# Attention with 64-key blocks for 58 queries, and reciprocals spread as three bf16 parts

## The chip, the cores and the metric

The kernel runs on one core of a Trainium2 chip. The metric is the device time of one execution in microseconds (us). Fast executions of one kernel mostly agree within 1 to 2%; some fall into a slower state. The profile shows one execution on its engines: PE is the matrix engine (TensorE), PEld its weight loads, DVE is VectorE, ACT ScalarE, POOL GpSimd, SP the engine that issues loads.

## The reference

Attention over batch 8, 8 heads, 576 positions, head size 64, in two forms whose results are added. One attends in full on positions averaged four by four (144 of them); the other only to neighbours less than four positions away. The sum, as 4608 rows of 512, goes through a two-layer network with a SiLU between.

```python
out_d = sm_attn(q_d, k_d, v_d)                 # q_d, k_d, v_d: means of 4 positions
out_up = np.repeat(out_d, factor, axis=2)      # factor = 4
mask = np.abs(pos[:, None] - pos[None, :]) < factor
scores = np.where(mask, scale * np.matmul(q, k.transpose(0, 1, 3, 2)), -1e9)
out_local = np.matmul(softmax(scores), v)      # (cut: the softmax is written out)
x = (out_up + out_local) as [4608, 512]        # (cut: transpose and reshape)
h = x @ w_in                                   # 512 -> 2048
return (h * (1.0 / (1.0 + np.exp(-h)))) @ w_out
```

## The kernel before

Heads are handled in 32 pairs. The local band of a head is cut into key blocks of 64, each of which serves 48 queries, six blocks for half a head. All products of attention are 64x64 matmuls on quarters of the array (64*64 in the profile, where the network's have 128*128). A "visit" `V(n)` holds everything that TensorE does for attention between two portions of the network:

```python
def V(n):                                  # cut to its order
    pe_cross(u, pv, z)                     # PV of pair n-2 and Z of pair n-1: parts across halves
    pe_S(u, n)                             # scores of pair n
    pe_T(u, n + 1)                         # transposes of pair n+1
    pe_main(u, pv, z)                      # Z of pair n-1, then PV of pair n-2
    after_T(n + 1); after_PV(pv); after_Z(z); after_S(n)   # work of the other engines

for i in range(6):                         # in pe_S; the values (PV) have the same six blocks
    for h in range(2):
        for y in range(2):
            t = 288 * y + 48 * i
            mm(u, AB[half(y), h, 48 * i:48 * i + 48], kT[j][half(h), t:t + 64],
               qT[j][half(h), t:t + 48], rl, [rAB[h]])
```

Z, the denominators, are collected 36 columns at a time in rows of a bank. VectorE takes their reciprocal, and each row must then be spread over the 64 partitions of a head. The first four pairs (`NDIR = 4`) do it with matmuls (`RB`), all later ones by a round trip: written to DRAM, then read back twice, each read repeating one row over 64 partitions. ScalarE issues both steps, so it waits in its own stream until the write has landed before it can issue the reads (5.7 us for pair 4).

```python
def after_Z(p):
    one("DVE", f"r{p}", 0.75, lambda e: e.reciprocal(zr[i][:, :, :], CD[:, :, 360:396]), ...)
    if p < NDIR:
        return
    dma("ACT", f"z{p}", scr[u][:, :], zr[i]..., ...)          # write
    for h in range(2):
        dma("ACT", f"b{p}", Rb[u][half(h), :], src, ...)      # read, stride 0 over 64 partitions

def RB(p):
    for x in range(2):
        for m in range(10):                # float32 matmul against a selector
            mm(u, HP[:, x, 36 * m:36 * m + 36], sel[:, m, :], zr[i][:, x, :], ...)
    one("ACT", f"eb{p}", 0.8, ...)         # copy HP to Rb
```

The reciprocal, the copies out of PSUM, `th` (a tanh by ScalarE) and `gT` (its product by VectorE) all belong to chains that TensorE waits for: each g1 matmul group (four matmuls of the input layer) writes one of two banks `HP`, which is free again when `th` and `gT` have read it.

The softmax here doesn't subtract the row's maximum and nothing guards it: scores larger than these inputs give would overflow.

## Time and profile before

| | before |
|---|---|
| median (lowest to highest of 3) | 436.39 us (433.86 to 438.46) |
| profiled execution | 444.3 us, span 442.6, granted clock 0.942, of the slow state |
| matmuls of one visit | 160 |
| matmuls of RB, four pairs | 160 recorded passes, 35.0 us busy |
| instruction queue (queue 8) | 51 packets, 0.84 MB, so 16 KB each; TensorE has 13,090 recorded instructions (6530 matmuls, 6560 weight loads), 257 a packet: an instruction block |

The span is read in four stages, because each has another limit: up to the first g1 (65.9 us), then to the Z of the tenth visit (50.7), to the Z of the last pair (235.3), and the tail of the network alone (90.7). The lines are in the prediction.

### The profile page before, as it was taken

What the parts mean: (1) busy time and instruction counts of PE and PEld (TensorE: products, weight loads), DVE (VectorE), ACT (ScalarE), POOL (GpSimd) and SP (SyncE); (2) the same over time, 40 slices, a digit from 0 to 9 for tenths busy, and PEclk for the clock granted to TensorE, in tenths of its full rate; (3) what the DMA queues carried; (4) which work ended last, traced back from release to release, by engine and by line L of the source; (5) the groups of instructions that cost most, each with busy time, mean ns of one, the idle gap of its engine ahead of it and who ended that gap; (6) DMA issues with size and microseconds to landing.
All of it is one profiled execution on the core that took longest, in us unless ns stands there. A gap on an engine that the chain in (4) does not pass through costs nothing.

```text
span 442.6 us, 14638 instructions
## 1 busy us (share of the span) xinstructions
PE 384.9 (87%) x6530; PEld 265.3 (60%) x6560; DVE 221.0 (50%) x355; ACT 169.1 (38%) x290; POOL 166.2 (38%) x207
## 2 busy tenths in 40 slices
PE   2799987974597887969797989799999999999997
PEld 1799985653464554646465656466666656666653
DVE  5532125576555464656464656566776543433420
ACT  4221024532244251524344445354545434343421
POOL 9441224356634444445354545445632120000000
PEclk9999999889589896969698999999999999999999
DMA  8999909978997474746575767583131210110111
GB/s 224 262 275 279 211 8 204 254 184 238 215 269 208 125 219 123 198 141 187 146 191 160 204 185 221 152 209 111 67 97 63 87 62 28 43 49 24 49 47 71
DMA packets 87258, 67.35 MB, mean 152 GB/s; under 512 B 59036, under 2 KB 68764, under 8 KB 87196
## 3 DMA queue, kind: packets, MB, share of 16 engines
q1 hardware_dynamic: 74460, 48.77, 41.9%
q10 hardware_dynamic: 8512, 11.36, 9.1%
q0 software_dynamic: 4224, 6.29, 6.6%
q8 instruction: 51, 0.84, 0.8%
q14 instruction: 11, 0.09, 0.1%
HBM read 58.03 MB, written 10.47 MB: 155 GB/s over the span
## 4 chain that ended last, share of the span: by engine, by line
PE 82%; issue 7%; DMA 4%; DVE 2%; ACT 2%; ACTq 1%; SPq 0%; DVEq 0%
PE HP L336 40%; PE o L336 23%; PE CD L336 8%; PE pe_ L336 6%; DMA scr<-zr 2%; PE AB L336 2%; PE pe_ L526 1%; DMA Rb<-scr 1%; DMA qk<-in_k_dram 1%; ACTq L425 1%; PE o L526 1%; ACT th L738 1%; DVE zr L666 1%; DVE gT L740 0%; SPq L425 0%
## 5 line engine op out<-in xcount | busy, mean ns | idle before, releaser
L336 PE MATMUL HP<-xT,w_in_sb 128*128 128x512 f32 x576 | 177.7, 447 | 2.7 <-DVE gT L740 2.3
L740 DVE SCALAR_TENSOR_TENSOR gT<-th,HP 128x512 bf16<-128x512 f32 x144 | 97.1, 685 | 119.3 <-ACT th L738 118.8
L738 ACT ACTIVATE th<-HP 128x512 f32<-128x512 f32 x144 | 85.8, 598 | 160.1 <-PE HP L336 150.1
L336 PEld LDWEIGHTS HP<-xT,w_in_sb 128*128 128x128 f32 x576 | 114.4, 204 | 34.1 <-DVE gT L740 3.2
L336 PE MATMUL o<-w_out_bf,gT 128*128 128x512 bf16 x437 | 106.4, 386 | 2.5 <-issue 1.0
L336 PEld LDWEIGHTS o<-w_out_bf,gT 128*128 128x128 bf16 x464 | 42.0, 100 | 60.0 <-issue 17.6
L722 POOL TENSOR_TENSOR xT<-xo 128x576 fp32r<-128x576 f32 (+3 forms) x48 | 45.0, 950 | 74.0 <-DVE xo L695 74.0
L508 POOL CAST vb<-vs 128x768 bf16<-128x768 f32 x32 | 26.4, 826 | 97.5 <-PE CD L336 88.5
L666 DVE RECIPROCAL zr<-CD 128x72 f32<-128x72 f32 x32 | 19.4, 607 | 50.9 <-PE CD L336 50.9
L502 POOL CAST qkb<-qk 128x1152 bf16<-128x1152 f32 x30 | 34.4, 1146 | 25.1 <-PE pe_ L526 13.2
L336 PE MATMUL CD<-Pt,vb 64*64 64x48 bf16 x768 | 14.8, 196 | 24.7 <-issue 24.4
L336 PE MATMUL HP<-zr,gT 128*128 128x36 f32 x160 | 35.0, 408 | 0.2 <-DVE zr L666 0.2
L336 PEld LDWEIGHTS HP<-zr,gT 128*128 128x128 f32 x160 | 34.4, 332 | 0.6 <-DVE zr L666 0.3
L695 DVE TENSOR_TENSOR xo<-CD,Rb 128x720 f32<-128x720 f32 x32 | 28.7, 898 | 11.7 <-PE CD L336 9.7
L513 POOL TENSOR_TENSOR vt<-vq 128x512 f32<-128x512 f32 x24 | 30.8, 1283 | 0.0
L536 ACT ACTIVATE kT<-pe_ 128x576 bf16<-128x576 bf16 x32 | 20.8, 650 | 18.9 <-PE pe_ L526 11.2
L755 ACT ACTIVATE osb<-o 128x512 f32<-128x512 f32 x29 | 17.4, 599 | 26.4 <-PE o L336 26.2
L336 PEld LDWEIGHTS CD<-Pt,vb 64*64 64x64 bf16 x768 | 11.1, 117 | 26.5 <-issue 25.4
L336 PE MATMUL pe_<-w_out_bf,gT 128*128 128x512 bf16 x109 | 26.1, 380 | 0.2
L540 DVE TENSOR_REDUCE kd<-kT 128x144 bf16<-128x576 bf16 x32 | 23.6, 738 | 1.7 <-ACT kT L536 1.7
L526 PE MATMUL o<-idn,qkb 64*64 64x64 bf16 x576 | 17.8, 206 | 7.6 <-DVE qkb L497 6.0
L543 DVE TENSOR_REDUCE qd<-qT 128x144 bf16<-128x576 bf16 x32 | 23.8, 743 | 1.3 <-ACT qT L339 1.2
(69 smaller groups left out, 358.3 us busy)
## 6 DMA issues: line engine op xcount, KB each, us to landing
vs<-in_v_dram SPq DMA_DIRECT2D x126, 96.0 KB, 4.1
Rb<-scr ACTq DMA_DIRECT2D x56, 180.0 KB, 4.1
qk<-in_q_dram SPq DMA_DIRECT2D x32, 288.0 KB, 5.5
out_dram<-osb SPq DMA_DIRECT2D x36, 256.0 KB, 2.3
qk<-in_k_dram SPq DMA_DIRECT2D x31, 288.0 KB, 6.0
vq<-in_v_dram SPq DMA_DIRECT2D x24, 256.0 KB
w_in_sb<-in_moe_w_in_dram POOLq DMA_DIRECT2D x4, 1024.0 KB, 10.0
w_out_bf<-in_moe_w_out_dram POOLq DMA_DIRECT2D x4, 512.0 KB, 9.9
```

The lines of the kernel that those rows point to most:

```text
L336: L.op(u, lambda t: t.matmul(out_, lhsT, rhs, start=start, stop=stop, skip_group_check=True), r, w)
L502: one("POOL", f"c{p}", 1.15, lambda g: g.tensor_copy(qkb[j][:, :, :], qk[i][:, :, :]), r=[R(f"qk{i}0"), R(f"qk{i}1")], w=[R(f"qkb{j}0"), R ...
L508: one("POOL", f"cw{p}", 0.85, lambda g: g.tensor_copy(vb[m][:, :, :], vs[i][:, :, :]), r=rr, w=[R(f"vb{m}")])
L513: one("POOL", f"va{p}", 1.3, lambda g: g.tensor_tensor(vt[:, :, :], vq[i][:, :, 0:128], vq[i][:, :, 128:256], ALU.add), r=rr, w=[R("vt")])
L526: L.op(u, lambda e, o=o, w=w, j=j: e.transpose(o, w, idn[half(j), :]), [R("id"), R(f"qkb{n}{x}")], [rE if x else rF])
L540: one("DVE", f"mk{p}", 0.74, lambda e: e.tensor_reduce(kd[j][:, 0:SD], kT[j][:, 8:584].rearrange("p (g r) -> p g r", r=4), AX.X, ALU.add), ...
L543: one("DVE", f"mq{p}", 0.74, lambda e: e.tensor_reduce(qd[j][:, :], qT[j][:, :].rearrange("p (g r) -> p g r", r=4), AX.X, ALU.add), r=[R(f ...
L666: one("DVE", f"r{p}", 0.75, lambda e: e.reciprocal(zr[i][:, :, :], CD[:, :, 360:396]), r=rCD, w=[R(f"zr{i}")], prio=-4)
L695: one("DVE", f"m{p}", 0.92, lambda e: e.tensor_tensor(xo[x][:, :, :].rearrange("p x (m n) -> p x m n", n=36), CD[:, :, 0:360].rearrange("p ...
L722: one("POOL", f"a{p}", 0.15 + n * 0.0019, lambda g, dst=dst, in0=in0, in1=in1: g.tensor_tensor(dst, in0, in1, ALU.add), r=[R(f"xo{x}")], w ...
L738: one("ACT", f"t{j}_{f}", 0.62, lambda e: e.activation(th[tb][:, :], hps[hb], AF.Tanh, scale=0.5), r=[rH[hb]], w=[R(f"th{tb}")], prio=-1)
L740: one("DVE", f"s{j}_{f}", 0.71, lambda e: e.scalar_tensor_tensor(gT[j % 2][:, f, :], th[tb][:, :], 1.0, hps[hb], ALU.add, ALU.mult), r=[rH ...
```

## The change

Its intent is fewer instructions on TensorE, and no float32 matmuls. A key block of 64 can serve 58 queries (three neighbours on each side), so five blocks do instead of six: a visit has 4 matmuls fewer for scores and 4 fewer for values. Z is collected 72 columns at a time instead of 36, 28 matmuls fewer: 124 a visit, not 160. The reciprocal then has 144 columns instead of 72. RB writes the reciprocal as a sum of three bf16 numbers and spreads each with a bf16 selector.

```diff
-            for i in range(6):                      # pe_S; PV likewise
+            for i in range(5):
-                        t = 288 * y + 48 * i
-                        mm(u, AB[half(y), h, 48 * i:48 * i + 48], kT[j][half(h), t:t + 64],
-                           qT[j][half(h), t:t + 48], rl, [rAB[h]])
+                        c, n = 58 * i, 58 if i < 4 else 56
+                        t = 288 * y + c
+                        mm(u, AB[half(y), h, c:c + n], kT[j][half(h), t:t + 64],
+                           qT[j][half(h), t:t + n], rl, [rAB[h]])
 ...
-                for s in range(8):                  # Z in pe_main; the other Z parts likewise
+                for s in range(4):
-                            mm(u, CD[half(h), j, 360:396], ..., Pt[m][half(j), h, 36 * s:36 * s + 36], ...)
+                            mm(u, CD[half(h), j, 360:432], ..., Pt[m][half(j), h, 72 * s:72 * s + 72], ...)
 ...
-            ... e.reciprocal(zr[i][:, :, :], CD[:, :, 360:396])
+            ... e.reciprocal(zr[i][:, :, :], CD[:, :, 360:432])
             if p < NDIR:
+                rh: h = bf16(zf);  rx: rest = zf - h;  rm: m = bf16(rest);  rl: l = bf16(rest - m)   # four DVE ops
                 return
 ...
-            for x in range(2):                      # RB
-                for m in range(10):
-                    mm(u, HP[:, x, 36 * m:36 * m + 36], sel[:, m, :], zr[i][:, x, :], ...)
+            for m in range(5):
+                x, c = divmod(m, 3)
+                for a in range(3):
+                    mm(u, HP[:, x, 144 * c:144 * c + 144], sel[:, m, :], rpart[a], ...,
+                       start=a == 0, stop=a == 2)
```

Cut: the windows in which values are loaded (80 KB instead of 96), masks, constants (their fills moved from GpSimd to VectorE), the value sums of a pair on TensorE (`VP`, 14 matmuls instead of 16), two value casts moved to ScalarE, and the estimated costs that the kernel's own scheduler orders by.

## The prediction

> **What bounds the kernel now.** I read the page first (busy shares, slices, the chain), then the groups of matmuls by form, the list of waits, the busy times by stage, and last the timeline of TensorE around two visits. A "visit" is the block of small 64x64 matmuls for attention: scores of one pair, transposes of the next, denominators (Z) of the one before and values (PV) of the one before that. From the tenth visit on, four groups of input-layer matmuls (g1) and four of output-layer matmuls (g2) stand between visits.
>
> The page: TensorE is busy 87% of the span, and the chain that ended last is 82% TensorE with 7.2% "issue", time in which nothing that the profile shows was waited for. The three rows of section 2 say when: TensorE is full in the tail, but near the middle has slices of 4 to 8 and a granted clock of 5 to 9.
>
> ```profile
> PE 384.9 (87%) x6530; PEld 265.3 (60%) x6560; DVE 221.0 (50%) x355; ACT 169.1 (38%) x290; POOL 166.2 (38%) x207
> PE   2799987974597887969797989799999999999997
> PEclk9999999889589896969698999999999999999999
> q8 instruction: 51, 0.84, 0.8%
> PE 82%; issue 7%; DMA 4%; DVE 2%; ACT 2%; ACTq 1%; SPq 0%; DVEq 0%
> L336 PE MATMUL HP<-zr,gT 128*128 128x36 f32 x160 | 35.0, 408 | 0.2 <-DVE zr L666 0.2
> L336 PEld LDWEIGHTS HP<-zr,gT 128*128 128x128 f32 x160 | 34.4, 332 | 0.6 <-DVE zr L666 0.3
> ```
>
> The last two rows are the spreading of the first four pairs' reciprocals (RB): 160 float32 passes, 35 us, with no wait. The stage view (columns: length, then busy us of PE, PEld, DVE, ACT, POOL, clock, DMA share, GB/s) cuts the span at the first g1 (65.9), at the Z of the tenth visit (116.6) and at the Z of the last pair (351.9):
>
> ```profile
> 0.00:65.90 65.90, 53.42 (x937) 50.42 (x937) 22.39 (x41) 15.18 (x24) 26.80 (x59) 1.00 0.93 211
> 65.90:116.60 50.70, 36.06 (x1011) 27.43 (x1008) 31.38 (x55) 20.87 (x37) 29.51 (x31) 0.85 0.96 221
> 116.60:351.90 235.30, 208.55 (x4114) 136.20 (x4128) 136.89 (x216) 100.35 (x175) 107.42 (x117) 0.92 0.58 161
> 351.90:442.60 90.70, 86.90 (x492) 51.22 (x500) 30.30 (x44) 32.66 (x55) 2.44 (x2) 1.00 0.13 49
> ```
>
> Then the gaps. Two rows of the list of waits:
>
> ```profile
> PEld CD L336 <- issue: 28.5, 17, 4.6
> PE CD L336 <- issue: 24.4, 9, 4.5
> ```
>
> and the timeline of one visit with a gap in it (start, duration, instruction, wait before it):
>
> ```profile
> 212.01 0.30 PE L336 MATMUL CD<-Pt,vb 64*64 64x48 bf16 x14
> 215.04 0.36 PE L336 MATMUL CD<-Pt,vb 64*64 64x48 bf16 x10 [2.73 <-issue]
> 215.18 0.36 PE L336 MATMUL CD<-Pd,vd 64*64 64x72 bf16 x8
> 215.46 3.78 PE L336 MATMUL HP<-xT,w_in_sb 128*128 128x512 f32 x8
> ```
>
> The reader is to see a run of equal matmuls broken in the middle, with no semaphore involved, and the eight g1 matmuls after it at 3.71 us on the chain instead of 1.85 us. Such gaps begin at 141.3, 164.4, 188.6, 212.3, 235.8, 257.8, 277.7 and 298.6 us, always 766 recorded TensorE instructions apart, and sum to 22.6 us. Z to Z, visits alternate between 8.9 us (no gap) and 11 to 15.4 us. So stage 3 is not bound by matmuls: its 22 visits would take 22 x 8.9 = 196 us, and it takes 235.
>
> [...] 766 is three blocks, and in the gap at 212.31 the packet starts at 212.39, takes 1.03 us, and TensorE goes on at 215.04. [...]
>
> **The change, part by part.**
>
> *RB in bf16.* Removed: 4 x 40 float32 passes at 217 ns = 4 x 8.7 us, all on the path between 15 and 62 us. Added: 4 x 15 bf16 matmuls of 144 columns, [...] 1.8 to 3 us per pair. TensorE is given back about 25 us. VectorE gets a reciprocal of 144 columns: [...] 1.08 us, so 0.5 us more; and four small operations of about 0.25 us, 1 us a pair. Then the chain of a pair binds: Z, reciprocal, PV, multiply on the same two banks take about 0.5 + 1.1 + 0.5 + 0.9 us [...], and the VectorE sum of a pair is about 5.6 us (two reductions 1.5, mask 0.45, reciprocal 1.1, parts 1.0, two value copies 0.6, multiply 0.9). I take 6.5 us a pair. First Z at about 14 us as before (two value casts moved to ScalarE may make it wait for their loads; the constants come earlier), fourth Z at 33.5, then reciprocal, parts, RB, copy, multiply, add: 1.1 + 1.2 + 2.5 + 1.2 + 0.9 + 1.2 and hand-overs, about 10 us. First g1 at 44 us, not 65.9.
>
> *Stage 2, first g1 to tenth Z.* Instructions there fall from 2240 to 1736 (counted in the compiled order, two for a matmul). Before, 50.7 us for 8.8 blocks is 5.8 us a block[...]: the gaps at 101, 106, 112 and 118 us lie in 992 small instructions in a row (now 772). In proportion: 39 us. But visits here also wait for the round trip of the reciprocals through DRAM, and the DMA work that had its rest at 55 to 66 us (8 GB/s in that slice) now has none. I take 44 us: tenth Z at 88. The loads allow it: about 21 MB must be in by then, at some 250 GB/s 84 us.
>
> *Stage 3.* A visit loses 36 of 160 matmuls. Without a gap, 160 take about 1.5 us and the pace is about 8 ns each at 36 as at 48 columns, so 0.3 us; columns per quadrant stay the same, and 72 columns are a little slower, so 0.25 us. The larger gain is the gaps. Visit plus g1 and g2 were 320 + 64 = 384 instructions, one and a half blocks, so every second visit held a whole block (0 slow instructions in it); now 248 + 64 = 312, and a visit is shorter than a block. Counting slow g1/g2 instructions in each block of the compiled order, placed where the old gaps fall: before 0, 64, 64 repeating, with 0 nine times; now 14 to 19 in four blocks, and 40 or more in all others. 16 slow ones last 16 x 0.115 = 1.8 us, so a gap of 2.8 us on average shrinks to about 1 us: four of them. Against that VectorE has 0.5 us more per visit, in front of the operations that free the g1 banks (VectorE about 7 us of 8.7): 0.1 us. So 22 x (8.9 - 0.25 + 0.1) = 192.5, and 6 us for leftover gaps and cold matmuls: 198.5 us.
>
> *Stage 4* is untouched: 90.7 us.
>
> *Off the path:* value windows of 80 KB instead of 96 (a sixth fewer 256-byte pieces), value casts shorter, the write of reciprocals 72 KB instead of 36, constants moved from POOL to VectorE in the first 4 us.
>
> Sum: 44 + 44 + 198.5 + 90.7 = 377.2 us, and 1.7 us between span and time (444.3 against 442.6): **379 us**. From a median of 436.39 that is a factor of 0.87: 22 from stage 1, 7 from stage 2, 37 from stage 3 on the profile's own terms. The profiled execution was 8 us slower than the median, which I put to longer gaps; the new kernel has few, so I take nothing off.
>
> **The rivals.** *Only TensorE's work counts.* 25 us from RB and 30 visits x 0.3 us: 436 - 34 = about 402 us. For: the gaps are nowhere explained by a semaphore, so they might stay. Against: their period of 766 and the packet inside each.
> *The gaps move.* [...] if the four short blocks and some others still wait 2 to 4 us and TensorE goes cold again, stage 3 is 212 us: about 392.
> *DMA or the queue that issues takes over.* Stages 1 and 2 already have DMA shares of 0.93 and 0.96. If their bytes (about 25 MB) set the pace at 220 GB/s, tenth Z is at 105 to 110 and the time about 398. For: the shares. Against: the loads had run four pairs ahead and stood still at 55 to 66.
> *VectorE becomes the bound of a visit:* 7 us of 8.7 leaves room, but in-order pile-ups could cost 0.5 us a visit: 388.
> *Better than thought:* stage 2 in proportion and no gap left: about 368.
>
> **Range and chances.** Four of the five rivals lie above 379, so the range is wider upward: 366 to 397. Every version, even the worst, is over 2% faster: 0.98, with 0.015 for within 2% and 0.005 for slower.
>
> **What would show it.** RB: 60 matmuls, 7 to 12 us in all. First g1 at 40 to 48; tenth Z at 83 to 95. Reciprocal about 1.1 us. Z to Z in stage 3 about 8.7 us nearly everywhere, no alternation; "issue" before CD down from 24 us to some 5 to 10; granted clock of stage 3 at 0.97 or more; queue 8 with about 41 packets. Wrong if gaps of 2 to 4 us keep coming every few visits, if g1 waits for VectorE for more than a few us, or if stage 2 stays near 50 us with DMA at its share of 0.96.

## The result, and the profile after

| | before | after |
|---|---|---|
| median | 437.42 us | 390.39 us |
| lowest to highest of 4 | 433.86 to 443.36 | 388.85 to 391.66 |
| ratio | | 0.8948 (0.8876 to 0.9019) |

A ratio here is the mean time of one kernel's fast runs over that of the other's fast runs of the same rounds, so not quite the ratio of the medians. The prediction was 379 us with a range of 366 to 397: faster, inside the range, 11 us too low. The profiled execution of after (span 389.9, clock 0.943) is a fast one. That of before was slow, so differences of the two profiles add up to 52.7 us where the medians differ by 47; which stage holds the other 6 us, one profile of before cannot tell.

The page of after. As before: busy times, TensorE's slices and its granted clock in them, the queue of instruction blocks, the shares of the chain.

```profile
PE 337.1 (86%) x5262; PEld 219.8 (56%) x5292; DVE 239.5 (61%) x395; ACT 169.1 (43%) x296; POOL 159.1 (41%) x199
...
PE   2587497545699998999989999899999999999996
PEclk9998668985599999999999999999999999999999
...
q8 instruction: 41, 0.67, 0.7%
...
PE 68%; DMA 15%; SPq 6%; issue 3%; DVE 3%; ACTq 2%; ACT 2%; POOL 1%; POOLq 0%; DVEq 0%
```

TensorE's busy time fell by 48 us, from 384.9 to 337.1, and the whole right side of the slices is now full, at full clock. The holes are all in the first eleven slices, up to 107 us. The chain tells the same: "issue" is down from 7% to 3%, and DMA is up from 4% to 15%.

The stages of after (from:to and length, then busy us of PE, PEld, DVE, ACT, POOL, then clock, DMA share, GB/s; a share over 1 means that packets overlap on an engine):

```profile
0.00:41.60 41.60, 23.55 (x713) 18.72 (x713) 29.70 (x82) 18.09 (x32) 20.92 (x50) 0.96 1.03 274
41.60:101.70 60.10, 36.57 (x788) 26.76 (x784) 33.93 (x54) 19.36 (x35) 31.08 (x32) 0.71 1.05 229
101.70:299.50 197.80, 190.32 (x3326) 123.39 (x3341) 145.21 (x216) 99.04 (x175) 104.72 (x117) 0.99 0.68 185
299.50:389.90 90.40, 86.66 (x460) 50.98 (x468) 30.67 (x44) 32.66 (x55) 2.43 (x2) 1.00 0.13 49
```

| stage | before | predicted | after |
|---|---|---|---|
| 1, to the first g1 | 65.9 | 44 | 41.6 |
| 2, to the tenth visit's Z | 50.7 | 44 | 60.1 |
| 3, to the last pair's Z | 235.3 | 198.5 | 197.8 |
| 4, tail | 90.7 | 90.7 | 90.4 |

Three stages came near what was predicted. Stage 2 was to become 7 us shorter and became 9 us longer, although its work is smaller: 788 matmuls instead of 1011. Its clock fell from 0.85 to 0.71, and its DMA share rose from 0.96 to 1.05. TensorE was busy for as long as before (36.6 us, before 36.1), and its idle time, the length less the busy time, grew from 14.6 to 23.5 us. (The clock of stage 1 is hardly a measurement: the traces hold no clock event before 70.9 us in before and 28.8 us in after.)

The groups by form show the parts that were priced (count, then busy us and mean ns of one, then idle time before them), and the list of waits what is left of "issue" before CD:

```profile
L339 PE MATMUL HP<-gT 128*128 128x144 bf16 x60 | 7.8, 299 | 1.5 <-DVE gT L681 1.2
...
L673 DVE RECIPROCAL zr<-CD 128x144 f32<-128x144 f32 x32 | 33.8, 1056 | 8.3 <-PE CD L339 8.3
```

```profile
PEld CD L339 <- issue: 12.7, 29, 2.7
...
PE CD L339 <- issue: 3.0, 3, 2.6
```

RB takes 7.8 us where it took 35.0. The reciprocal takes 1056 ns (607 before at half the columns). The two rows of waits were 28.5 and 24.4 us.

Where do the 60 us of stage 2 go? The largest waits of TensorE in it (total, times, longest) are:

```profile
PE CD L339 <- DVE vd L603: 7.8, 2, 5.3
PE HP L339 <- POOL xT L736: 4.3, 2, 3.0
PE CD L339 <- DVE xo L709: 3.9, 1, 3.9
```

Of the first, 5.3 us (at 88.05) stand behind the round trip: in VectorE's order a `gT` comes before `vd`, and its `th` stood on ScalarE behind the write. With 1.9 us for a `gT` at 62.05, shown below, that makes 7.3 us directly behind the trip (2.0 before). The other 2.5 us of the first and the third end after VectorE has gone through a reciprocal, a copy, two reductions and a multiply without pause; such waits were there before too (3.0 and 3.5). The second is new: `xT`, the input of g1, stands in GpSimd's order behind casts that wait for loads of values (for 1.9 and 0.8 us just before). A further 4.3 us is "issue" (2.6 before).

The chain of waits of after from 41 to 103 us has the write of reciprocals to DRAM (`scr<-zr`) with 22.9%, g1 and RB matmuls on HP with 19.8%, "issue" with 9.4%, the reads (`Rb<-scr`) with 8.3% and loads of values with 8.1%. One piece of it (start, duration, what):

```profile
53.77 5.69 DMA scr<-zr
59.48 0.50 ACTq L426
60.02 0.61 ACTq L426
60.67 0.61 ACT th L752
61.30 0.70 DVE gT L754
62.05 1.39 PE HP L339 x4
```

and ScalarE's timeline at two places (start, duration, operation, idle time before it):

```profile
53.77 0.34 ACTq L426 DMA_DIRECT2D scr<-zr  x1
...
59.48 1.14 ACTq L426 DMA_DIRECT2D Rb<-scr  x2
60.67 0.60 ACT L752 ACTIVATE th<-HP 128x512 f32<-128x512 f32 x1 [2.53 <-PE HP L339]
...
168.70 0.34 ACTq L426 DMA_DIRECT2D scr<-zr  x1
...
173.38 1.10 ACTq L426 DMA_DIRECT2D Rb<-scr  x2
174.58 0.60 ACT L769 ACTIVATE osb<-o 128x512 f32<-128x512 f32 x1 [3.96 <-PE CD L339]
```

The reader is to see one engine used for two things. The write is issued at 53.77 and lands 5.69 us later. Only then, at 59.48, does ScalarE issue the reads, and what it has to compute next, the `th` that frees a bank for TensorE, starts at 60.67. The row gives PE as its releaser, but TensorE had long been done; what ScalarE stood for was the write. Four matmuls of g1 follow at 62.05. The write takes 5.7, 6.7, 6.2 and 2.3 us for pairs 4 to 7 (before: 5.7, 6.8, 2.7 and 3.0), and from the write's issue to the landing of the reads it is 13.6, 13.3, 12.7 and 8.0 us. For pair 4 that was 13.8 us before: the single trip has hardly become slower.

The lower half shows the same at 173.38, in stage 3: the copy of an output bank starts at 174.58 after 3.96 us of idleness, and TensorE's transposes, which need that bank, wait 0.83 us. In stage 3 of after TensorE has five gaps of over 0.4 us, at 146.8, 174.4, 202.1, 219.5 and 246.6 us, 5.0 us in all (1.18, 0.83, 0.74, 0.72, 1.54). At every one ScalarE has just issued reads and was idle for 3.6 to 4.8 us before its next operation. None is one of the old instruction gaps.

### The profile page after: what moved, and what is told of

The parts are those of the page before. It is cut to its first block, busy times and chain, and to the rows that moved or that the text cites.

```text
span 389.9 us, 12145 instructions
## 1 busy us (share of the span) xinstructions
PE 337.1 (86%) x5262; PEld 219.8 (56%) x5292; DVE 239.5 (61%) x395; ACT 169.1 (43%) x296; POOL 159.1 (41%) x199
## 4 chain that ended last, share of the span: by engine, by line
PE 68%; DMA 15%; SPq 6%; issue 3%; DVE 3%; ACTq 2%; ACT 2%; POOL 1%; POOLq 0%; DVEq 0%
PE HP L339 32%; PE o L339 21%; DMA scr<-zr 10%; PE pe_ L339 7%; SPq L426 6%; PE CD L339 5%; DMA vs<-in_v_dram 4%; ACTq L426 2%; PE AB L339 2%; DMA Rb<-scr 1%; DVE gT L754 1%; PE o L531 1%; PE pe_ L531 1%; DVE zr L673 1%; ACT th L752 1%
## 5 line engine op out<-in xcount | busy, mean ns | idle before, releaser
L339 PE MATMUL HP<-xT,w_in_sb 128*128 128x512 f32 x576 | 167.7, 430 | 8.9 <-DVE gT L754 4.6
L754 DVE SCALAR_TENSOR_TENSOR gT<-th,HP 128x512 bf16<-128x512 f32 x144 | 96.7, 685 | 114.4 <-ACT th L752 114.1
L339 PEld LDWEIGHTS HP<-xT,w_in_sb 128*128 128x128 f32 x576 | 109.7, 196 | 39.0 <-DVE gT L754 6.4
L339 PE MATMUL o<-w_out_bf,gT 128*128 128x512 bf16 x437 | 102.2, 380 | 2.2 <-DVE qT L342 0.3
L339 PEld LDWEIGHTS o<-w_out_bf,gT 128*128 128x128 bf16 x464 | 42.2, 98 | 56.8 <-issue 6.4
L513 POOL CAST vb<-vs 128x640 bf16<-128x640 f32 x30 | 21.5, 717 | 73.6 <-PE CD L339 59.2
L673 DVE RECIPROCAL zr<-CD 128x144 f32<-128x144 f32 x32 | 33.8, 1056 | 8.3 <-PE CD L339 8.3
L541 ACT ACTIVATE kT<-pe_ 128x576 bf16<-128x576 bf16 x32 | 20.9, 653 | 17.0 <-PE pe_ L531 10.5
L531 PE MATMUL o<-idn,qkb 64*64 64x64 bf16 x576 | 17.5, 206 | 10.4 <-DVE qkb L498 5.6
L339 PE MATMUL CD<-Pd,vd 64*64 64x72 bf16 x384 | 16.1, 213 | 11.8 <-DVE vd L603 7.8
L548 DVE TENSOR_REDUCE qd<-qT 128x144 bf16<-128x576 bf16 x32 | 23.8, 743 | 0.0
L573 ACT ACTIVATE Pt<-AB 128x576 bf16<-128x576 f32 x32 | 20.7, 648 | 4.6 <-PE AB L339 4.6
L339 PEld LDWEIGHTS CD<-Pd,vd 64*64 64x64 bf16 x384 | 9.3, 112 | 22.6 <-issue 9.7
L531 PEld LDWEIGHTS o<-idn,qkb 64*64 64x64 bf16 x576 | 14.4, 120 | 11.2 <-DVE qkb L498 6.5
```

The costliest lines, as they stand in the source:

```text
L339: L.op(u, lambda t: t.matmul(out_, lhsT, rhs, start=start, stop=stop, skip_group_check=True), r, w)
L531: L.op(u, lambda e, o=o, w=w, j=j: e.transpose(o, w, idn[half(j), :]), [R("id"), R(f"qkb{n}{x}")], [rE if x else rF])
L548: one("DVE", f"mq{p}", 0.74, lambda e: e.tensor_reduce(qd[j][:, :], qT[j][:, :].rearrange("p (g r) -> p g r", r=4), AX.X, ALU.add), r=[R(f ...
L673: one("DVE", f"r{p}", 1.2, lambda e: e.reciprocal(zr[i][:, :, :], CD[:, :, 360:432]), r=rCD, w=[R(f"zr{i}")], prio=-4)
L754: one("DVE", f"s{j}_{f}", 0.71, lambda e: e.scalar_tensor_tensor(gT[j % 2][:, f, :], th[tb][:, :], 1.0, hps[hb], ALU.add, ALU.mult), r=[rH ...
```

## The experiments

Ratios are against before, medians in us; stage lengths and the time of the tenth Z (the end of stage 2) are from each run's profile. The cut between stages 1 and 2 moves with the first g1, so where runs differ in stage 1, the tenth Z is the fairer measure. The runs were made in four sessions and on more than one chip.

| run | median | ratio | stage 1 | 2 | tenth Z | stage 3 |
|---|---|---|---|---|---|---|
| after | 390.39 | 0.8948 | 41.6 | 60.1 | 101.7 | 197.8 |
| three parts for nine pairs | 391.94 | 0.8974 | 42.6 | 60.0 | 102.6 | 196.3 |
| before, 64 instructions more | 426.37 | 0.9774 | 65.9 | 56.8 | 122.7 | 214.1 |
| bf16 RB alone | 408.91 | 0.9362 | 50.2 | 56.1 | 106.3 | 210.3 |
| blocks of 58 alone | 409.16 | 0.9362 | 66.4 | 53.0 | 119.4 | 196.4 |
| light weights (wrong) | 380.70 | 0.8637 | 44.3 | 47.1 | 91.4 | 196.9 |
| reads issued later | 387.72 | 0.8814 | 41.0 | 57.5 | 98.5 | 197.6 |
| two parts for nine pairs | 382.92 | 0.8660 | 45.8 | 47.1 | 92.9 | 201.7 |
| 12 pairs sum values on TensorE | 394.09 | 0.8938 | 40.3 | 61.4 | 101.7 | 200.0 |
| two parts, light weights (wrong) | 376.03 | 0.8664 | 41.7 | 45.1 | 86.8 | 199.1 |

Theory A for stage 2 was: the round trip of the reciprocals, slowed by the loads, binds. Rivals: VectorE's longer chains, ScalarE's order of work, and the loads by themselves. For stage 3 the theory was that the old gaps are instruction blocks arriving late, with the number of small instructions in a row as the cause; the rival, that a visit simply has less work.

### No round trip for the first nine pairs, three parts

```diff
-NDIR = 4
+NDIR = 9
         Z(4)
+        RB(4)
             V(n)                 # n = 6..9
+            RB(n - 1)
```

> The changed kernel, with the reciprocals of pairs 4 to 8 spread by bf16 matmuls too, so that no round trip through DRAM is left between the first g1 and the tenth Z. Theory A (stage 2 is held by the round trip: in the changed kernel the write of the reciprocals lands after 5.7, 6.4 and 6.2 us, with ScalarE standing before the reads): stage 2 falls from 60 us to about 40 [...], time about 371 us. Theory B (stage 2 is held by the bytes that the DMA has to bring in, some 25 MB by the tenth Z): 2 MB less changes it by under 8 us, time about 383. Theory C (instruction fetch alone): 150 instructions more than in the changed kernel, stage 2 about 63 us, time about 393.

Stage 2 did not move (60.0 us; time 391.94, ratio 0.8974, 0.891 to 0.9038). The expectation's theory C, instruction fetch, named the nearest numbers (63 and 393 us); theory A (40 us, an estimate) missed by 20. Taken alone this speaks against theory A. But the stage is now bound by something else. Its line (as the stage lines above):

```profile
42.60:102.60 60.00, 41.02 (x851) 30.74 (x851) 41.54 (x72) 23.56 (x45) 31.50 (x33) 0.76 0.90 214
```

and a stretch of its chain:

```profile
60.48 1.06 DVE zr L673
61.54 0.61 DVE qd L548
62.15 0.14 DVE gT L678
62.29 0.66 DVE kd L545
62.95 0.73 DVE gT L679
63.68 0.60 DVE gT L754
```

VectorE works without a pause here: reciprocal, a reduction (qd), a part of the reciprocal (L678, which lies in gT's buffer), a reduction (kd), the next part (L679), the product of the network (L754). Its busy time in the stage rose from 33.9 to 41.5 us, and the DMA share fell to 0.90. TensorE's waits for `vd` and `xo` fell from 11.7 to 1.2 us; those for VectorE's `gT`, the parts of the reciprocal included, rose from 2.4 to 10.4, and the 4.0 us for `xT` stayed. So one wait was taken away and another put in its place, and this run cannot say what the trip cost.

### The kernel before with 64 instructions more, once

```diff
             if n < NPAIR:
                 pe_S(u, n)
+            if n == 9:
+                pe_S(u, n)       # the same scores a second time; result unchanged
```

> The kernel before, with the 32 score matmuls of the ninth visit issued twice (same result): 64 instructions more, once, just before stage 3. Theory A (the gaps are instruction blocks that hold no slow instruction, every third one by the accident of alignment): the shift leaves at least 20 slow instructions in nearly every block of stage 3; the gaps of 2 to 4.5 us vanish, visits take 8.9 us throughout, stage 3 about 201 us and the time about 411. Theory B (the gaps come from DMA load, from the two visits' semaphores or from the amount of instructions as such): nothing changes, time 436 to 439.

The edit only adds work, and the kernel became faster: 426.37 us, ratio 0.9774 (0.9704 to 0.9845; below 1, but not clearly by 2%). Stage 3 went from 235.3 to 214.1 us, with the matmuls of its visits unchanged:

```profile
122.70:336.80 214.10, 201.51 (x4118) 130.78 (x4128) 136.28 (x216) 100.13 (x175) 107.31 (x117) 0.97 0.62 174
```

```profile
PEld CD L336 <- issue: 8.5, 11, 3.4
...
PE CD L336 <- issue: 5.1, 3, 3.2
```

The "issue" before CD was 28.5 us for weight loads and 24.4 for matmuls (the same gaps seen by two engines, so not to be added); it is 8.5 and 5.1 here. By the edit, what moved is only where block boundaries fall against the runs of small matmuls (a block of some 257 instructions, by the page of before); that this is what shortened the gaps is read from it, as nothing else in the visits changed. Leftover gaps of 0.5 to 2.1 us remained, 10.7 us in stage 3 by the trace, so theory A's 201 us and 411 us were not reached. The time gained 10 us and not 21: stage 2 became 6 us longer, and the slow state of before's profile may account for the rest.

### Each half of the change alone

bf16 RB alone, on the kernel before (visits keep 160 matmuls):

```diff
-            for x in range(2):
-                for m in range(10):
-                    mm(u, HP[:, x, 36 * m:36 * m + 36], sel[:, m, :], zr[i][:, x, :], ...)   # float32
+            for m in range(10):
+                x, c = divmod(m, 5)
+                for a in range(3):
+                    mm(u, HP[:, x, 72 * c:72 * c + 72], sel[:, m, :], rpart[a], ...)         # bf16
```

> The kernel before (blocks of 48 queries, 160 matmuls a visit) with the bf16 reciprocals alone: 30 matmuls of 72 columns per pair in place of 40 float32 passes. First g1 at about 42 to 44 us. Theory A (alignment): 80 instructions fewer before stage 3 shift the blocks too, and only some five early blocks there hold 4 to 19 slow instructions, so stage 3 falls to about 205 us although a visit still has 160 matmuls, and the time is about 400. Theory B (the gaps need fewer matmuls per visit): stage 3 stays at about 230 us and the time is about 415 to 420.

Blocks of 58 alone, on the kernel after (RB back to float32):

```diff
-            for m in range(5):
-                x, c = divmod(m, 3)
-                for a in range(3):
-                    mm(u, HP[:, x, 144 * c:144 * c + 144], sel[:, m, :], rpart[a], ...)
+            for x in range(2):
+                for m in range(5):
+                    for s in range(2):
+                        c = 72 * m + 36 * s
+                        mm(u, HP[:, x, c:c + 36], sel[:, m, :], zr[i][:, x, 36 * s:36 * s + 36], ...)
```

> The changed kernel with its reciprocals of the first four pairs spread in float32 again, 20 matmuls (40 passes) per pair as before. First g1 at 62 to 66 us. Stage 3 as in the changed kernel, 198 us. Theory A (the long first stage lets loads run ahead, so stage 2 is then short again): stage 2 about 42 to 48 us, time about 402. Theory B (stage 2 is long in the changed kernel for a reason inside it, such as the longer reciprocal or its larger write): stage 2 stays at 60 us, time about 415.

With bf16 RB alone the first g1 came at 50.2 us, not at the expected 42 to 44; with blocks of 58 alone stage 2 took 53.0 us, between its two theories. Either half gave a ratio of 0.9362, 6.4% each; both together give 10.5%, not 12.8%. Two things follow.

First, stage 3 with the old visits of 160 matmuls takes 210.3 us when the rest of the program is 80 instructions shorter, and 214.1 when it is 64 longer, against 235.3. In both runs the clock of the stage is 0.97 or more (0.92 before). So of the 37.5 us that after gains in stage 3, 21 to 25 belong to where the old kernel's blocks happened to lie, and 12.5 to 16.3 (210.3 or 214.1 less 197.8) remain. The smaller visit does not have all of these: gaps of over 0.4 us still sum to 9.7 and 10.7 us in the two runs and to 5.0 in after, which leaves some 8 to 11 us for it. Up to 6 us of the first share may be the slow state in which before was profiled.

Second, stage 2 takes 53.0 us where stage 1 takes 66.4, 56.1 where it takes 50.2, and 60.1 where it takes 41.6. What stage 1 saves, stage 2 gives back in part: this is why the halves do not add. With blocks of 58 alone, where the loads have the long stage 1 to run ahead, TensorE never waits for `xT` or "issue" in stage 2, but 10.6 us behind the round trip.

### Fewer bytes of weights

To see whether the loads matter, three quarters of both weight matrices are not loaded, and matmuls use the first quarter again. The result is wrong (relative error 1.74); the instructions stay the same.

```diff
         for c, t in enumerate((10, 14, 18, 22, 34, 38, 42, 46)):
-            load_w(c).ready = float(t)
+            if c in (0, 4):
+                load_w(c).ready = float(t)
-  w_in_sb[:, kc, 128 * f:128 * f + 128], ... w_out_bf[:, f, :]
+  w_in_sb[:, kc, 128 * (f % 4):128 * (f % 4) + 128], ... w_out_bf[:, f % 4, :]
```

> The changed kernel with only the first quarter of each MoE weight loaded and used four times over (the output is wrong on purpose; every instruction of TensorE, VectorE and ScalarE is as in the changed kernel). 3.1 MB of w_in and 1.6 MB of w_out less, of the 25.1 MB that the changed kernel has brought in by its tenth Z at 101.7 us. Theory A (stages 1 and 2 together are held by those bytes, 247 GB/s on average): tenth Z at 82 to 86 us, time about 373. Theory B (stage 2 is held by its chain of visits, ScalarE, VectorE and the blocks of instructions): tenth Z at 97 us or later, time 386 or more.

380.70 us (2 runs), ratio 0.8637 (0.8573 to 0.8702). The tenth Z comes at 91.4 us, 10.3 earlier: between the two theories, which said 82 to 86 and 97 or later. Stage 2 falls to 47.1 us:

```profile
44.30:91.40 47.10, 31.71 (x784) 23.73 (x784) 33.31 (x54) 19.76 (x37) 24.95 (x25) 0.84 0.92 228
```

and the same piece of ScalarE's timeline as above, the write and reads of pair 4:

```profile
51.19 0.36 ACTq L426 DMA_DIRECT2D scr<-zr  x1
...
53.94 1.14 ACTq L426 DMA_DIRECT2D Rb<-scr  x2
```

The write lands after 2.7 us, not 5.7. That piece is not typical: the next writes take 3.1, 6.2, 2.4 and 5.0 us (after: 6.7, 6.2, 2.3 and 4.8), and TensorE's longest wait behind the trip is no shorter, 5.6 us (after: 5.3). What is gone are the waits for `xT` (4.3 us, now none) and most of "issue" (4.3 us, now 1.0); and at a clock of 0.84 instead of 0.71 the same matmuls keep TensorE busy for 31.7 us instead of 36.6. So the loads that run beside it cost the way to the tenth Z 10 us, but at most in a small part by way of the round trip. They are needed, so this is no version to keep.

### The same work, ordered as if the write took longer

The kernel's own scheduler orders each engine's stream by estimated costs and took the write to land in about 1.8 us. Here it is told 4 us more for the first nine pairs, so that other ScalarE work goes ahead of the reads.

```diff
-                u.end = ring[e] + 1.6
+                u.end = ring[e] + 1.6 + u.extra
-            dma(eng, f"z{p}", scr[u][:, :], zf, ...)
+            dma(eng, f"z{p}", scr[u][:, :], zf, ...).extra = 4.0 if p < 9 else 0.0
```

> The changed kernel with the scheduler told that the write of the reciprocals takes 4 us longer for pairs 4 to 8, so that ScalarE's order has other work (tanh for g1) between the write and the reads; nothing else changes. Theory A (DMA bytes): the tenth Z stays within 3 us of 101.7. Theory B (ScalarE standing 5.7 to 6.4 us behind the write, in order, is what lengthens stage 2): tenth Z at 90 to 95 us, time about 381.

Stage 2 took 57.5 us and the time was 387.72, ratio 0.8814 (0.8722 to 0.8906), which the interval does not separate from after's. In the chain of stage 2 the write is gone from the top, and the reads have taken its place with 23.8% (8.3% in after). The tenth Z comes 3 us earlier (98.5; theory B said 90 to 95): with the reads later, the multiply that needs them waits instead. TensorE's wait for `vd` is gone, and that for `xo` is 11.7 us, as much as both were.

### No round trip for nine pairs, with two parts

Of the three parts the last is dropped. VectorE has two operations fewer for each of these pairs and RB five matmuls fewer.

```diff
-NDIR = 4
+NDIR = 9
-  rh, rx, rm, rl                      # h, rest, m, l
+  rh, rx                              # h, and m = bf16(zf - h) written directly
-                for a in range(3):
+                for a in range(2):
         (RB(4) after Z(4), RB(n - 1) after V(n) for n = 6..9, as in the first experiment)
```

> The earlier variant with bf16 spreading for nine pairs, with two bf16 parts in place of three (two VectorE operations and five matmuls less per pair, about 0.6 us of VectorE each). In that variant the DMA had only 138 GB/s between 80 and 103 us and the chain ran over VectorE. Theory A (VectorE and its order hold that variant's stage 2): five pairs times 0.6 to 1 us, tenth Z at 96 to 99 us, time about 387. Theory B (bytes hold it too): tenth Z stays at 102 us, time 391.

The result is correct, the time 382.92 us (379.33 to 386.74), ratio 0.866 (0.8577 to 0.8744). It is the fastest correct version, and beats both kernels (all its runs lie below after's lowest, though on another chip). Its profiled execution was slow (386.74); even so, stage 2 was 47.1 us and the tenth Z at 92.9, earlier than either theory had it (96 to 99, or 102):

```profile
45.80:92.90 47.10, 34.26 (x788) 25.32 (x788) 32.30 (x57) 21.76 (x41) 27.26 (x28) 0.83 1.00 233
```

Against the first experiment, which also had no round trip, VectorE's busy time in the stage is 32.3 instead of 41.5 us, and the tenth Z 9.7 us earlier. Against after, with nearly the same VectorE time (33.9), it is 8.8 us earlier: the waits for `vd` and `xo` are 1.7 us instead of 11.7, and those for `gT` 7.1 instead of 2.4. So the trip had cost time there all along, hidden in the first experiment by the VectorE work that replaced it.

### Value sums of twelve pairs on TensorE

The downsampled values of the first eight pairs are formed by TensorE (`VP`), those of later pairs by GpSimd from a second load of 320 KB. Twelve instead of eight pairs saves four such loads.

```diff
-NVP = 8
+NVP = 12
             if n < NPAIR + 2:
+                if n - 2 < NVP:
+                    VP(n - 2)
                 V(n)
```

> The changed kernel with the value sums of pairs 8 to 11 made by matmuls from the windows already loaded, not from a second load of the values: 1.3 MB less for the DMA and 2 us less of GpSimd per pair, 28 instructions more of TensorE in each of four visits. Theory A (bytes): tenth Z 4 to 6 us earlier, at 96 to 98 us, time 385 to 387. Theory B (visits' chain): tenth Z stays at 102 us, and the extra matmuls make stage 3 some 2 us longer, time about 392.

394.09 us, ratio 0.8938 (0.889 to 0.8985), not told apart from after. Stage 2 is 61.4 us with a DMA share of 0.96; by the tenth Z 24.5 MB had moved (241 GB/s for 101.7 us) and not 25.1. So, as theory B had it, 0.6 MB fewer bytes did not shorten it, though 18 more matmuls stand in it. Stage 3 became 2 us longer.

### Splitting the visit (three runs with wrong results)

The idea was to shorten the rows of small instructions in stage 3: cross parts, scores and transposes first, then two g1 and two g2 groups, then the rest.

```diff
-                V(n)
+                Va(n)            # pe_cross, pe_S, pe_T
             ...                  # G1, g2, G1, g2
+            Vb(n)                # pe_main, after_PV, after_Z
```

On the kernel with two parts:

> The two-part variant with every visit of stage 3 cut in two: scores and transposes (144 instructions), then two g1 and two g2 groups, then denominators and values (104), then the rest. The instructions are the same in kind and number, only their order differs: each block of stage 3 now holds at least 32 slow instructions, where the changed kernel has blocks with 14 to 19 and the two-part variant with 7 to 11. Theory A (the last gaps of stage 3 are short blocks too): stage 3 falls from 198 to 202 us to about 190 (22 visits of 8.6 us), time about 373. Theory B (what is left there comes from VectorE or from DMA): no change or, since the values come some 4 us later, a little slower, time about 383 to 386.

On the kernel after:

> The changed kernel with the same cut of the visits in stage 3 and nothing else. Theory A: stage 3 from 198 to about 190 us, stage 2 as it was (60 us), time about 382 to 384. Theory B: 390 or more.

On the first of these, with the write again taken to land 2 us later:

> The split two-part variant with the scheduler told that each write of the reciprocals takes 2 us longer, so that ScalarE does a tanh before it stands waiting to issue the reads. If ScalarE's waits cost anything in stage 3 the time falls by 2 to 4 us against the split variant; if not it stays within 1 us.

They took 384.33, 395.45 and 390.06 us (ratios 0.8851, 0.9083 and 0.9014), and all three results are wrong. `Va` already marked the pair's values as used, so the cast that overwrites them was placed before `Vb`, which still reads them. No race check sees this, since the two are ordered, only in the wrong order; and it adds a wait of its own. They decide nothing about stage 3.

### Two parts and light weights together

The last of a set of four: trip or no trip, full or light loads (again wrong). The edit is the two edits above.

> The two-part variant (no round trip through DRAM before the tenth Z) with only a quarter of the weights loaded, as in the earlier light run; the output is wrong on purpose. In the changed kernel the lighter load took 10 us off the tenth Z. Theory A (the load hurts through the round trip of the reciprocals): with no round trip there the lighter load gains little, tenth Z at 90 to 93 us. Theory B (the load hurts by the loads themselves, which come late): tenth Z at about 83 us.

376.03 us (2 runs), ratio 0.8664 (0.8393 to 0.8936). Its tenth Z came at 86.8 us, between the two theories (90 to 93, about 83). Beside the other three, in us (stage 2 in brackets):

| tenth Z | full loads | light loads |
|---|---|---|
| round trip (three parts for four pairs) | 101.7 (60.1) | 91.4 (47.1) |
| no round trip (two parts for nine pairs) | 92.9 (47.1) | 86.8 (45.1) |

By the length of stage 2 it would seem that either is slow only together with the other: the loads cost 13 us with the trip and 2 without it. But the first g1 came at 41.6, 44.3, 45.8 and 41.7 us, so the cut moved. By the tenth Z the loads cost 10.3 us with the trip and 6.1 without; the trip costs 8.8 us with full loads and 4.6 with light ones. Each costs something alone. Together they cost some 4 us more than the sum, in one profile each, one of them slow; by the ratios, 0.866 and 0.8664, the lighter loads gave nothing once the trip was gone, but the interval of the last is too wide to tell. That they slow each other is therefore not shown.

## Why the prediction was right, and where it was off

The direction, the range and the lengths of three of the four stages held; the sum was 11 us low because the term for stage 2 was mis-sized.

- *RB in bf16.* Predicted 7 to 12 us in all; it measured 7.8. From first matmul to last the four pairs take 3.5, 2.6, 2.0 and 1.1 us (1.8 to 3 predicted, an estimate). The last two never pause, and the last takes little more than half of the one before it: the third, 1.98 us from 32.17, lies in a stretch for which the trace has a granted clock of 0.50 (32.2 to 35.6 us), the last, 1.11 us from 35.82, in one at 1.00 (35.6 to 42.4). The reciprocal is 1056 ns (1080 predicted, an estimate), and the four operations that make the parts take 482, 304, 343 and 302 ns on average, 1.4 us a pair (1 predicted).
- *Stage 1.* First g1 at 41.6 us (44 predicted), but not by the path of the prediction, which had a pair's work on VectorE set a pace of 6.5 us, with Z at about 14, 20.5, 27 and 33.5. The reciprocals of the four Z start at 15.6, 18.7, 28.4 and 32.3 us, and the chain of the stage is 58.1% SP issuing loads and 34.1% loads of values (before: 52.8% matmuls on HP). The length came right partly by luck: by the chain, loads and their issue bound stage 1, as one of the rivals had it. No run tests this; with fewer weights alone the first g1 came no earlier (44.3).
- *Stage 2*, the term "I take 44 us: tenth Z at 88". It measured 60.1, tenth Z at 101.7. This is the step that failed, in both of its parts. It shrank the stage in proportion to its instructions, to 39 us; but TensorE was busy 36.6 us with 788 matmuls, no less than before with 1011 (36.1), at a granted clock of 0.71 instead of 0.85. (Its 5.8 us a block are only the length of the stage by its instructions: that a fetch takes so long is not shown, and the seven packets of queue 8 that start in stage 2 of before take 0.96 to 2.06 us.) And it allowed 5 us for the round trip and the missing rest of the DMA work together; but TensorE stood idle for 23.5 us, of which 7.3 directly behind the round trip, 6.4 behind VectorE's row of work after a Z (6.5 before), 4.3 behind late loads of values and only 4.3 in "issue". The prediction's own sign of being wrong, a stage 2 near 50 us with DMA at 0.96, was surpassed (60.1, 1.05). The trip was on the chain before as well: its write had 19.2% of the chain in stage 2, which the prediction had not sized. And it took 21 MB to be needed by the tenth Z; 25.1 MB had been moved by then, in before and in after alike. Among the rivals, "DMA or the queue that issues takes over", with the tenth Z at 105 to 110, was nearer for this stage, though not for the kernel (398).
- *Why it got longer, not only less short.* What before had in stage 1 was time for loads: 35 us of RB, during which they ran ahead until they stood still (8 GB/s in the slice from 55.3 to 66.4 us). The table of the halves shows stage 2 growing as stage 1 shrinks. TensorE's idle time grew by 9 us: 5.3 more behind the round trip, 4.3 for `xT` behind value loads, 1.7 more of "issue", and some 2 less elsewhere. The waits for `xT` and most or all of "issue" go away when the loads have time (blocks of 58 alone) or are fewer (light weights); those for `xT` are also gone in the two-part version, where the first g1 came 4 us later. The waits behind the trip do not: 10.6 us with blocks of 58 alone, and one of 5.6 with light weights; they go with the trip itself (two parts). So two causes stand side by side, and where the trip is gone, VectorE's `gT` is next, which is one reason why the gains do not add. Not settled is what of the trip counts. It is its latency in ScalarE's order, or its own bytes too: five writes of 72 KB and four pairs of reads of 180 KB, 1.8 MB by the tenth Z, are 7.5 us of DMA time at after's 247 GB/s. Against bytes alone stands the run with 4.7 MB fewer weights, which at that rate should have gained 19 us and gained 10, and the one with 0.6 MB fewer, which gained none. Nor is it settled why "issue" falls with the loads.
- *Stage 3.* 198.5 predicted, 197.8 measured; queue 8 has 41 packets, as predicted; clock 0.99. The cause, gaps of instruction blocks, rests on the 64 added instructions (gaps of 22.6 us became 10.7 with the same visits) and on the packets named below. How much slow instructions in a block shorten its gap was an estimate. Unlike what the prediction took, the four weak blocks show no gap: in stage 3 "issue" leaves none over 0.4 us. The 5.0 us of gaps that remain (6 predicted) are ScalarE standing behind the round trip. The amount was right, for another reason; that this reason holds is read from the trace and was not tested, because the splits failed. The smaller visits were to give 3.5 us (196 less 192.5) and gave more, some 8 to 11. (In a visit of before at full clock, from 225.5 us, 28 matmuls of 36 columns follow one another at 8.6 ns, 24 of 48 columns at 7.9 and 8 of 72 columns at 22.) Z to Z is within 0.1 us of 8.6 in 11 of 22 visits and 7.6 to 11.5 in the others, not 8.7 "nearly everywhere", though the alternation is gone.
- *Stage 4* and "VectorE becomes the bound of a visit": 90.4 us, untouched. In stage 3 VectorE did not become the bound (145 of 198 us busy).
- *Two readings of the prediction.* "The packet inside each" gap holds for seven of the eight (for the sixth in part); in the last, at 298.6, none lies. And the cold matmuls that it counts with: after the gap at 212.3 the eight g1 matmuls took 3.71 us against 1.85, and the trace has a granted clock of 0.50 from 214.3 for 6.8 us. Such a stretch, of 3.4 or 6.8 us, begins in or just after each of the first five gaps (4.46, 4.12, 3.18, 2.73 and 2.62 us), none at the last three (1.78, 2.91 and 0.78).

## What to carry to other kernels

Before crediting a gain to less work, add a few harmless instructions: if the kernel gets faster, as here (64 of them, and stage 3 went from 235.3 to 214.1 us), a part of its time may be only where instruction blocks fall. When an early stage is shortened, ask what ran under it for free (here, loads), because the next stage has to carry it; and look for every round trip through DRAM that some engine waits out in its own stream (here 3.6 to 4.8 us of ScalarE at each of the five gaps of stage 3). A run that removes a wait and does not get faster has not shown that the wait was cheap: look at what ended the idle time instead. And before saying that two costs feed each other, compare at a point in time that does not move with the cut between stages.
